# Rebuilding the opening of a fused attention and SwiGLU kernel: dummy products, a fixed order for four tiles, a shorter load front, and a merged unit for the cross blocks

## The chip, the cores and the metric

The kernel runs on one core of a Trainium2 chip. Times are device microseconds (us) of one execution. A quoted time is the median of several runs, and a ratio is the mean time of one kernel's fast runs over the mean time of the other kernel's fast runs in the same rounds on the same chip, so it isn't quite the ratio of the medians. "Span" is the length of the profiled execution as the trace has it; it is about 2 us shorter than the device time of the same run.

In the traces the clock granted to TensorE reads 1.00 or, in some stretches, 0.50. A product of 512 columns starts every 216 ns or every 415 ns; these are called full and half rate here. A group of four such products takes 0.86 or 1.66 us, and this is how the two states are told apart below.

## The reference

Attention over 8 batches of 576 positions, 8 heads of 64, each query looking back at most 127 positions with a linear bias, then a SwiGLU feed-forward network (FFN) over all 4608 rows.

```python
# q, k, v: (8, 8, 576, 64)
scores = (q @ k.T) / 8 + bias            # bias = -slope[h] * |i - j|
mask   = (i - j >= 0) & (i - j < 128)
x      = softmax(where(mask, scores, -1e9)) @ v     # -> (4608, 512)
# w_gate, w_val: (512, 1536), w_out: (1536, 512)
g   = x @ w_gate
out = (g * sigmoid(g) * (x @ w_val)) @ w_out        # fp32
```

## The kernel before

Two batches form a super-batch of nine units: four full tiles of 128 positions for each batch (576 = 4 x 128 + 64), and one corner tile that holds the last 64 rows of both. The FFN works in blocks of 512 rows: 12 gate groups and 12 value groups of four products each, then four output groups of 12 products. The output groups of one block run beside the gate and value groups of the next, and so do the attention tiles for later blocks. Four attention tiles must be done before the FFN can start, and these and the first FFN block are the opening that the change rebuilds.

All loads go through one queue that GpSimd feeds, and convert fp32 to fp16 on the way. The corner tile (rank 4) is loaded in two pieces of 64 rows, and it belongs to the first five tiles loaded:

```python
    def source(src, rank):
        s, c = divmod(rank, 9)
        if c == 4:                                # corner: two pieces of 64 rows
            return [((64 * n, 64 * n + 64),
                     src[2 * s + n, :, 512:576, :].rearrange("h p d -> p h d")) for n in range(2)]
    # ... cut
    load_qk(0, "kq")
    for r in range(4):
        load_qk(r + 1, "q")
        load_v(r)
        load_qk(r + 1, "k")
    load_w(0, 128)
    load_w(128, 512)          # gate and value weights by columns
    load(5)
    load_v(4)
    load_w(512, 1024)
    load(6)
    load_w(1024, 1536)
    load(7)
    load(8)
    # ... then wo_sb, the output weights, in two halves
```

Transposes, scores, weighted sums and the transposes of x all share one pool of four PSUM banks, `ps_a`. The FFN has its own four, which stand empty until it starts:

```python
    ps_f = ctx.enter_context(tc.tile_pool(name="ps_f", bufs=3, space=PSUM))   # gv x3, po x1
    ps_a = ctx.enter_context(tc.tile_pool(name="ps_a", bufs=4, space=PSUM))   # attention
    # ... cut
        pt = ps_a.tile([P, 4, P], FP16, name="pt", tag="a")
        for j in range(4):
            nc.tensor.transpose(pt[:, j, :], t_[:, 2 * j:2 * j + 2, :], idm)
        nc.vector.tensor_copy(dst[:, :, c * P:(c + 1) * P], pt)
```

The corner's queries need scores against tile 3 of the first batch, tile 3 of the second and the corner itself. Before, the first two of these ride along as the second 128 columns of units 3 and 7, with masks of their own (`lo`, `hi`), and unit 8 computes only the corner against itself.

The softmax here doesn't subtract the row's maximum and nothing guards it: scores larger than these inputs give would overflow.

Of the kernel before, what the change touches and what calls it, by code (L numbers as in the profile page):

```python
# [15 lines left out]
P = 128  # L16
WIN = 128
QK_DMA_FROM = 14
X_DMA_FROM = 99
FIRST = 4  # L20
# [21 lines left out]
def kernel(  # L42
# [24 lines left out]
    nc.sync.dma_start(idm, idm_d.ap())  # L67
    reg_d = nc.inline_tensor(make_mask(H), name="mask_reg")
    reg = consts.tile([P, H, 256], FP16, name="m_reg")
    nc.sync.dma_start(reg, reg_d.ap())  # L70
    lo = consts.tile([P, H, 256], FP16, name="m_lo")
    hi = consts.tile([P, H, 256], FP16, name="m_hi")
    com = consts.tile([P, H, 128], FP16, name="m_com")

    def make_lo():

        nc.vector.memset(lo[:, :, 192:256], 0.0)
        nc.vector.tensor_copy(lo[:, :, 0:192], reg[:, :, 0:192])

    def make_hi():  # L80

        nc.vector.memset(hi[:, :, 128:192], 0.0)
        nc.vector.tensor_copy(hi[:, :, 0:128], reg[:, :, 0:128])
        nc.vector.tensor_copy(hi[:, :, 192:256], reg[:, :, 128:192])

    def make_com():

        nc.vector.memset(com, 0.0)
        nc.vector.tensor_copy(com[0:64, :, 0:64], reg[0:64, :, 0:64])
        nc.vector.tensor_copy(com[64:128, :, 64:128], reg[64:128, :, 64:128])  # L90
# [18 lines left out]

    NV = 14  # L110
# [9 lines left out]

# [3 lines left out]

    def col_of(p):
        return p if p < 4 else (p + 1 if p < 8 else 4)
# [4 lines left out]
    def source(src, rank):  # L131

        s, c = divmod(rank, 9)
        if c == 4:
            return [((64 * n, 64 * n + 64),
                     src[2 * s + n, :, 512:576, :].rearrange("h p d -> p h d")) for n in range(2)]
        b, t = (2 * s, c) if c < 4 else (2 * s + 1, c - 5)
        return [((0, P), src[b, :, t * P:(t + 1) * P, :].rearrange("h p d -> p h d"))]
# [17 lines left out]
    def transposed(name, rank):  # L156

        s, c = divmod(rank, 9)
        t_, dst = (natk.pop(rank), kTs[s]) if name == "k" else (natq.pop(rank), qTs[s])
        pt = ps_a.tile([P, 4, P], FP16, name="pt", tag="a")  # L160
        for j in range(4):
            nc.tensor.transpose(pt[:, j, :], t_[:, 2 * j:2 * j + 2, :], idm)
        nc.vector.tensor_copy(dst[:, :, c * P:(c + 1) * P], pt)

    def transposes(rank):
# [4 lines left out]
        if rank >= QK_DMA_FROM:  # L170
            cols = slice(c * P, (c + 1) * P)
            for t_, dst in ((natk.pop(rank), kTs[s]), (natq.pop(rank), qTs[s])):
                nc.sync.dma_start_transpose(
                    dst[:, :, cols], t_.rearrange("p h d -> p (h d)"))
            return
        for name in ("kq" if c == 0 else "qk"):
            transposed(name, rank)
# [3 lines left out]
    def scores(i):  # L181

        s, p = units[i]
        c = col_of(p)
        kcols = slice(c * P, (c + 1) * P)
        kT, qT = kTs[s], qTs[s]
        if p == 8:
            banks = [ps_a.tile([P, 4, P], FP32, name="psc", tag="a") for _ in range(2)]
            for j in range(4):
                for par in range(2):  # L190
                    rows = slice(64 * par, 64 * par + 64)
                    nc.tensor.matmul(banks[par][:, j, :], kT[rows, j, kcols], qT[rows, j, kcols],
                                     start=(j == 0), stop=(j == 3))
            er = epool.tile([P, H, P], FP16, name="exrc", tag="exrc", bufs=1)
            e = epool.tile([P, H, P], FP16, name="exc", tag="exc", bufs=1)
            ex[(s, p)] = e

            er4 = er.rearrange("k (a par b) q -> k a par b q", a=2, par=2)

            def act(par):  # L200
                nc.scalar.activation(er4[:, :, par], banks[par].rearrange("k (a b) q -> k a b q", a=2),
                                     AF.Exp, scale=scale)

            return [[lambda: act(0)],
                    [lambda: act(1), lambda: nc.vector.tensor_mul(e, er, com)], [], []]

        banks = []
        for q4 in range(2):
            two = [ps_a.tile([P, 2, 256], FP32, name="ps", tag="a") for _ in range(2)]
            banks.append(two)  # L210
            for j in range(2):
                pair = 2 * q4 + j
                if p == 7:
                    parts = [(0, slice(8 * P, 9 * P)), (P, slice(4 * P, 5 * P))]
                else:
                    parts = [(0, slice(c * P, (c + 2) * P))]
                for n, (o, cols) in enumerate(parts):
                    w = cols.stop - cols.start
                    for par in range(2):
                        rows = slice(64 * par, 64 * par + 64)  # L220
                        nc.tensor.matmul(two[par][:, j, o:o + w], kT[rows, pair, kcols],  # L221
                                         qT[rows, pair, cols],
                                         start=(j == 0 and n == 0),
                                         stop=(j == 1 and n == len(parts) - 1))
        er = epool.tile([P, H, 256], FP16, name="exr", tag="exr", bufs=2)
        if p in (3, 7):
            e = epool.tile([P, H, 256], FP16, name="exl", tag="exl", bufs=2)
        else:
            e = epool.tile([P, H, 256], FP16, name="ex", tag="ex", bufs=3)
        ex[(s, p)] = e  # L230
        m = lo if p == 3 else hi if p == 7 else reg
# [5 lines left out]
        def mul(q4):  # L237
            o = slice(4 * q4, 4 * q4 + 4)
            nc.vector.tensor_mul(e[:, o, :], er[:, o, :], m[:, o, :])  # L239

        return [[lambda: act(0, 0)], [lambda: act(0, 1), lambda: mul(0)],
                [lambda: act(1, 0)], [lambda: act(1, 1), lambda: mul(1)]]

    xs = {}

    def weighted(i):
# [4 lines left out]
        for half in range(2):  # L251
            av = ps_a.tile([P, 4, D + 1], FP32, name="av", tag="a")
            todo = []
            for j in range(4):
                h = 4 * half + j
                if p == 8:
                    todo.append((j, ex[(s, 3)][:, slot(h), 128:256], va[9 * s + 3][:, h, :]))
                    todo.append((j, ex[(s, 7)][:, slot(h), 128:256], va[9 * s + 8][:, h, :]))
                    todo.append((j, ex[(s, 8)][:, slot(h), :], va[9 * s + 4][:, h, :]))
                else:  # L260
                    if p not in (0, 4):
                        todo.append((j, ex[(s, p - 1)][:, slot(h), 128:256],
                                     va[9 * s + col_of(p - 1)][:, h, :]))
                    todo.append((j, ex[(s, p)][:, slot(h), 0:128], va[9 * s + col_of(p)][:, h, :]))
# [14 lines left out]
    def x_transposed(i):  # L279
# [9 lines left out]
        pt = ps_a.tile([P, NKB, P], FP16, name="px", tag="a")  # L289
        for kb in range(NKB):  # L290
            nc.tensor.transpose(pt[:, kb, :], x[:, kb * P:(kb + 1) * P], idm)  # L291
# [54 lines left out]
    need_rank = [9 * s + r for s in range(NSUP) for r in (1, 2, 3, 4, 6, 7, 8, 8, 8)]  # L346
# [8 lines left out]
    def transposes_to(r):  # L355
        nonlocal done_t
        while done_t <= min(r, NR - 1):
            transposes(done_t)
            done_t += 1

    def ahead(i):

        r = min(need_rank[min(i + 4, last)], loaded - 1)
        if r >= QK_DMA_FROM:
            transposes_to(r)

    def attention():

        transposes_to(need_rank[0])
        for steps in scores(0):  # L370
            for f in steps:
                f()
        yield 0
        for i in range(last + 1):
            after = [[], [], [], []]
            if i < last and i != FIRST - 1:
                transposes_to(need_rank[i + 1])
                after = scores(i + 1)
            if i == 1:
                make_lo()  # L380
            if i == 5:
                make_hi()
                make_com()
            for fs in after:
                for f in fs:
                    f()
                yield i
            weighted(i)
            yield i
            if i >= FIRST:  # L390
                loads_to(i + 7)
                ahead(i)
# [4 lines left out]
            if i == FIRST - 1:  # L397

                transposes_to(need_rank[i + 1])
                for fs in scores(i + 1):  # L400
                    for f in fs:
                        f()
                    yield i + 1
# [7 lines left out]
    for r in range(4):  # L411
        load_qk(r + 1, "q")
        load_v(r)
        load_qk(r + 1, "k")
    load_w(0, 128)
    load_w(128, 512)
    load(5)
    load_v(4)
    load_w(512, 1024)
    load(6)  # L420
    load_w(1024, 1536)
# [8 lines left out]
    done = n_att = step = 0  # L430
# [10 lines left out]
    while done < ready[0]:  # L441
        att_step()
    base = n_att
    for _ in ffn():
        step += 1
        if step < 24:
            blk, target = 0, base + 2 * max(0, step - 8)
        else:
            blk = min(NBLK - 1, 1 + (step - 24) // 36)
            target = base + 32 + (step - 24) * RATE * 8 / 36  # L450
# [32 lines left out]
```

## Time and profile before

| | before |
|---|---|
| time, median (range) | 375.73 us (375.66 to 376.59, 3 runs) |
| span | 373.8 us |
| TensorE busy | 351.6 us, 94% of the span |
| share of the chain that ended last that is TensorE | 72% |
| FFN starts | 30.11 us |
| first output product (`po`) | 62.98 us |

TensorE is near its bound over the whole kernel; what can still be won is time near the start. The lines themselves are shown in the prediction. In a timeline line the columns are start, length, engine, line of the kernel, operation, output and inputs, shape, count, and in brackets the idle time before it and what released it.

### The profile page before, as it was taken

The numbers are of one execution on the slowest core, as the hardware profiler recorded it, in microseconds if no ns is written. First come the engines' busy times: TensorE is split into PE (matmuls) and PEld (weight loads), VectorE is DVE, ScalarE is ACT, GpSimd is POOL, SyncE is SP. The second block draws the span as 40 slices with busy tenths as digits, with TensorE's granted clock in tenths as the row PEclk, the third lists the DMA queues.
The fourth block names the chain that finished last, engine by engine and source line by source line (L and its number), as shares of the span: only waits on it lengthen the run. The fifth ranks groups of instructions, "written<-read, shape, count | busy, mean of one in ns | idle before, by whom it ended". The sixth has DMA issues, their size and how long they took to land.

```text
span 373.8 us, 6285 instructions
## 1 busy us (share of the span) xinstructions
PE 351.6 (94%) x2416; PEld 170.4 (46%) x2416; DVE 235.9 (63%) x471; ACT 173.4 (46%) x317; POOL 108.6 (29%) x134
## 2 busy tenths in 40 slices
PE   1789799999999999999999999999999999999995
PEld 1454345554445544444454444444454444444442
DVE  3765788765876488556865687568744833853540
ACT  1542475536655565456644575466433332332321
POOL 8966648755563654470000000000000000000000
PEclk9999999999999999999999999999999999999999
DMA  9999999999999999999001300010011002001013
GB/s 143 143 162 190 179 188 140 113 119 147 159 155 172 158 217 142 143 153 220 2 30 56 44 0 25 33 59 0 3 58 56 0 30 79 5 30 56 28 29 86
DMA packets 147806, 35.05 MB, mean 94 GB/s; under 512 B 138432, under 2 KB 143040, under 8 KB 147776
## 3 DMA queue, kind: packets, MB, share of 16 engines
q0 software_dynamic: 118304, 18.88, 77.2%
q1 hardware_dynamic: 29472, 15.77, 20.9%
q8 instruction: 19, 0.31, 0.4%
q14 instruction: 11, 0.09, 0.1%
HBM read 38.31 MB, written 9.44 MB: 128 GB/s over the span
## 4 chain that ended last, share of the span: by engine, by line
PE 72%; DVE 8%; DMA 7%; ACT 6%; POOL 4%; issue 2%; DVEq 0%; POOLq 0%
PE po L326 24%; PE pv L312 19%; PE pg L302 18%; ACT exr L235 5%; DMA qn<-in_q_dram 3%; PE ps L221 3%; PE av L266 3%; DMA wg_sb<-in_moe_w_gate_dram 3%; PE px L291 2%; DVE uu L307 2%; DVE hT L314 2%; DVE ex L239 2%; DMA kn<-in_k_dram 1%; POOL qn L149 1%; DVE x L269 1%
## 5 line engine op out<-in xcount | busy, mean ns | idle before, releaser
L307 DVE SCALAR_TENSOR_TENSOR uu<-tt,pg 128x512 f16<-128x512 f16 x108 | 74.0, 685 | 65.6 <-ACT tt L305 65.5
L312 PE MATMUL pv<-xT,wv_sb 128*128 128x512 f16 x432 | 113.5, 380 | 1.3 <-DVE uu L307 1.0
L302 PE MATMUL pg<-xT,wg_sb 128*128 128x512 f16 x432 | 112.4, 381 | 0.7 <-DMA va<-in_v_dram 0.7
L326 PE MATMUL po<-wo_sb,hT 128*128 128x512 f16 x432 | 103.5, 379 | 0.0
L305 ACT ACTIVATE tt<-pg 128x512 f16<-128x512 f32 x108 | 65.2, 603 | 80.3 <-PE pg L302 78.1
L314 DVE TENSOR_TENSOR hT<-uu,pv 128x512 f16<-128x512 f16 x108 | 74.1, 686 | 8.9 <-PE pv L312 1.1
L235 ACT ACTIVATE exr<-ps 128x512 f16<-128x512 f32 x128 | 67.0, 606 | 24.8 <-PE ps L221 24.8
L302 PEld LDWEIGHTS <-wg_sb 128*128 128x128 f16 x432 | 40.6, 98 | 45.7 <-issue 3.5
L312 PEld LDWEIGHTS <-wv_sb 128*128 128x128 f16 x432 | 40.5, 98 | 45.7 <-issue 4.6
L326 PEld LDWEIGHTS <-hT 128*128 128x128 f16 x432 | 40.1, 98 | 44.1 <-issue 1.9
L143 POOL DMA_DIRECT2D va<-in_v_dram x40 | 34.1, 865 | 48.2 <-PE av L266 41.9
L330 ACT ACTIVATE osb<-po 128x512 f32<-128x512 f32 x36 | 21.6, 600 | 56.1 <-PE po L326 56.0
L239 DVE TENSOR_TENSOR ex<-exr,m_reg 128x1024 f16<-128x1024 f16 x48 | 33.0, 689 | 19.0 <-ACT exr L235 18.9
L149 POOL DMA_DIRECT2D qn<-in_q_dram x40 | 34.0, 852 | 25.7 <-DMA qT<-qn 17.7
L149 POOL DMA_DIRECT2D kn<-in_k_dram x40 | 34.2, 857 | 24.8 <-DMA kT<-kn 17.3
L292 ACT COPY xT<-px 128x512 f16<-128x512 f16 x36 | 21.0, 585 | 33.9 <-PE px L291 33.6
L269 DVE TENSOR_TENSOR x<-av,rec 128x256 f16<-128x256 f32 x72 | 29.1, 420 | 0.8
L221 PE MATMUL ps<-qT,kT 64*128 64x256 f16 (+1 forms) x288 | 24.9, 274 | 0.3
L266 PEld LDWEIGHTS <-ex 128*128 128x128 f16 x384 | 19.1, 101 | 8.8 <-issue 2.4
L291 PE MATMUL px<-idm,x 128*128 128x128 f16 x144 | 19.3, 230 | 3.7 <-DVE x L269 3.0
L266 PE MATMUL av<-va,ex 128*128 128x65 f16 x384 | 20.9, 199 | 0.8 <-ACT exr L235 0.6
L291 PEld LDWEIGHTS <-x 128*128 128x128 f16 x144 | 10.1, 99 | 20.5 <-DVE x L269 17.0
(35 smaller groups left out, 115.0 us busy)
## 6 DMA issues: line engine op xcount, KB each, us to landing
out_dram<-osb SPq DMA_DIRECT2D x32, 256.0 KB, 2.1
kn<-in_k_dram POOLq DMA_DIRECT2D x32, 128.0 KB, 7.0
qn<-in_q_dram POOLq DMA_DIRECT2D x32, 128.0 KB, 7.1
va<-in_v_dram POOLq DMA_DIRECT2D x32, 128.0 KB, 7.3
wo_sb<-in_moe_w_out_dram POOLq DMA_DIRECT2D x2, 768.0 KB, 11.8
wg_sb<-in_moe_w_gate_dram POOLq DMA_DIRECT2D x2, 512.0 KB, 10.5
wv_sb<-in_moe_w_val_dram POOLq DMA_DIRECT2D x2, 512.0 KB, 11.6
out_dram<-osb SPq DMA_DIRECT2D x8, 128.0 KB, 2.4
```

Source lines behind the costliest of these rows:

```text
L149: nc.gpsimd.dma_start(t_[p0:p1], src)
L221: nc.tensor.matmul(two[par][:, j, o:o + w], kT[rows, pair, kcols], qT[rows, pair, cols], start=(j == 0 and n == 0), stop=(j == 1 and n == ...
L235: nc.scalar.activation(er[:, o:o + 2, :], banks[q4][par], AF.Exp, scale=scale)
L239: nc.vector.tensor_mul(e[:, o, :], er[:, o, :], m[:, o, :])
L266: nc.tensor.matmul(av[:, j, :], w, val, start=(n == 0), stop=(n == len(todo) - 1))
L291: nc.tensor.transpose(pt[:, kb, :], x[:, kb * P:(kb + 1) * P], idm)
L302: nc.tensor.matmul(pg, wg_sb[:, kb, ms], xT[n][:, kb, :], start=(kb == 0), stop=(kb == NKB - 1))
L305: nc.scalar.activation(tt, pg, AF.Tanh, scale=0.5)
L307: nc.vector.scalar_tensor_tensor(out=uu, in0=tt, scalar=1.0, in1=pg, op0=ALU.add, op1=ALU.mult)
L312: nc.tensor.matmul(pv, wv_sb[:, kb, ms], xT[n][:, kb, :], start=(kb == 0), stop=(kb == NKB - 1))
L314: nc.vector.tensor_mul(hT[(n, m)], uu, pv)
L326: nc.tensor.matmul(po, hT[(n, m)][:, j * P:(j + 1) * P], wo_sb[:, m, :], start=(m == 0), stop=(m == NMB - 1))
```

## The change

The intent is to start the FFN earlier, and to start it at full clock. It has five parts:

1. Twelve dummy products before the first data lands, and the transposes of the first four tiles done twice, to keep the clock up.
2. The first four tiles in a fixed order on TensorE, VectorE and ScalarE, in place of the scheduler's.
3. Banks of the FFN's pool for the transposes, weighted sums and x of these tiles.
4. The corner tile becomes rank 8 and leaves the front of the loads. v0 goes behind k1, and q5 before the second weight piece.
5. All three blocks of the corner's queries go into unit 8, each 128 wide; units 3 and 7 shrink to 128.

Beside these, the pacing of the attention changed: the score products of a unit became a step of their own, and in the first FFN block the attention sets in more slowly.

The diff, cut to its core:

```diff
+    def busy(n):
+        t_ = ps_f.tile([P, 512], FP32, name="nil", tag="po", bufs=1)
+        for _ in range(n):
+            nc.tensor.matmul(t_, idle[:, 0:P], idle, start=True, stop=True)
 ...
-        pt = ps_a.tile([P, 4, P], FP16, name="pt", tag="a")
-        for j in range(4):
-            nc.tensor.transpose(pt[:, j, :], t_[:, 2 * j:2 * j + 2, :], idm)
+        if rank < FIRST:
+            pt = ps_f.tile([P, 4, P], FP16, name="pt", tag="gv" if name == "k" else "po",
+                           bufs=3 if name == "k" else 1)
+        else:
+            pt = ps_a.tile([P, 4, P], FP16, name="pt", tag="a")
+        for _ in range(2 if rank < FIRST else 1):
+            for j in range(4):
+                nc.tensor.transpose(pt[:, j, :], t_[:, 2 * j:2 * j + 2, :],
+                                    idm if rank < FIRST else idm2)
 ...
+        if p == 8:
+            return sum([scores_128(s, kt, 8, (s, "c", n), msk[n]) for n, kt in enumerate((3, 7, 8))], [])
+        if p in (3, 7):
+            return scores_128(s, p, p, (s, p), reg[:, :, 0:P])
 ...
     load_qk(0, "kq")
-    for r in range(4):
-        load_qk(r + 1, "q")
-        load_v(r)
-        load_qk(r + 1, "k")
+    load_qk(1, "qk")
+    load_qk(2, "q")
+    load_v(0)
+    load_qk(2, "k")
+    load_qk(3, "q")
+    load_v(1)
+    load_qk(3, "k")
+    load_v(2)
+    load_v(3)
     load_w(0, 128)
     load_w(128, 512)
-    load(5)
-    load_v(4)
+    load(4)
+    load_qk(5, "q")
     load_w(512, 1024)
+    load_qk(5, "k")
+    load_v(5)
+    load_w(1024, 1536)
     load(6)
-    load_w(1024, 1536)
     load(7)
     load(8)
 ...
+        busy(WARM)                                      # WARM = 12
+        with tc.manual_schedule(engines=ENGINES[MANUAL]):   # PE, DVE, Activation
+            first_tiles()
+            done = FIRST
+            steps = enumerate(ffn(), 1)
+            while next(steps)[0] < ALONE:               # ALONE = 8: gates and values 0 to 3
+                pass
+            nc.scalar.copy(idm2, idm)
```

## The prediction

The forecast's sum: 5.25 less 0.7 gives 4.6, with 0.3 it is 4.9, and 375.7 - 4.9 = 370.8. The 372 of rival (b) is that sum with a cost at half rate added.

> **What bounds the kernel now.** I read the page first (busy tenths, chain), then the windows of the first 60 us, then the timelines of TensorE and GpSimd there, because the change touches only how the kernel opens.
>
> From the page, the busy tenths of TensorE and DMA, in 40 slices of 9.35 us, and the chain that ended last by engine:
>
> ```profile
> PE   1789799999999999999999999999999999999995
> ...
> DMA  9999999999999999999001300010011002001013
> ...
> PE 72%; DVE 8%; DMA 7%; ACT 6%; POOL 4%; issue 2%; DVEq 0%; POOLq 0%
> ```
>
> TensorE is full from the fourth slice to the end, except in the fifth. The chain is TensorE for 72%; what isn't TensorE lies in the opening. DMA is full for the first 19 slices. So every us by which TensorE's dense part starts earlier is a us off the end, but only if the data is there: two limits meet in the opening.
>
> TensorE's timeline there (start, length, engine, line, operation, count, idle before and its releaser):
>
> ```profile
> 19.24 1.06 PE L266 MATMUL av<-va,ex 128*128 128x65 f16 x16
> ...
> 30.11 1.86 PE L302 MATMUL pg<-xT,wg_sb 128*128 128x512 f16 x4 [0.67 <-DMA va<-in_v_dram]
> 31.77 1.32 PE L312 MATMUL pv<-xT,wv_sb 128*128 128x512 f16 x4
> 32.93 1.03 PE L302 MATMUL pg<-xT,wg_sb 128*128 128x512 f16 x4
> 33.79 1.03 PE L312 MATMUL pv<-xT,wv_sb 128*128 128x512 f16 x4
> ...
> 44.37 0.40 PE L162 MATMUL pt<-idm,qn 128*128 128x128 f16 x4 [1.93 <-DMA qn<-in_q_dram]
> ```
>
> Three things are to be seen. The FFN starts at 30.11, after four attention tiles that take about 5 us each. The first four gate products take 31.77 - 30.11 = 1.66 us, 415 ns each; later four take 33.79 - 32.93 = 0.86 us, 216 ns each: TensorE ran at half rate until about 32.5, though the granted clock reads 1.00. The two first groups lost 2.82 - 1.73 = 1.1 us to it. And at 42.4 TensorE stood for 1.93 us for a q tile. The chain in order of time says why, and the windows give the rates (the last two numbers are the mean share of the DMA engines, summed over queues, and GB/s as written):
>
> ```profile
> 21.55 10.71 DMA wg_sb<-in_moe_w_gate_dram
> 32.26 0.28 issue
> 32.54 11.78 DMA qn<-in_q_dram
> ```
>
> ```profile
> 8.00:10.00 2.00, 0.71 (x6) 0.45 (x7) 1.53 (x5) 0.00 (x0) 2.00 (x3) 1.00 2.42 154
> ...
> 36.00:38.00 2.00, 2.00 (x11) 0.93 (x10) 1.48 (x3) 0.87 (x2) 2.00 (x3) 1.00 1.32 203
> ```
>
> The queue serves transfers roughly in order: q, k and v tiles (128 KB as written) at 154 GB/s, 0.86 us each, equal to the 0.87 us that GpSimd takes to issue one; weight pieces of 512 KB at 203 GB/s, 2.6 us each. That q tile took 11.78 us because 1 MB of weights stood ahead of it.
>
> [...] A q, k or v row of one head is 64 fp32, 256 bytes, and moves at 154 against 203 GB/s. [...] The kernel uses 4 + 3 + 1, so four attention buffers were all that the opening had, while the FFN's four stood empty.
>
> **The change part by part.**
> *Dummies.* 12 products of 512 columns at half rate are 12 x 0.42 = 5 us, from about 1.2 to 6.2 or less: done when the first k tile lands (6.29). Cost nothing.
> *Loads.* The corner tile (k, q and v of the last 64 rows of two batches) leaves the front; v0 goes behind k1. The front is now 12 tiles, the first at 6.29, then each 0.87 later: k1 8.9, q3 12.4, k3 14.1, v3 15.9.
> *Fixed order and own banks.* I walked the instructions in their new order with the durations of before (copy 0.34 apart on VectorE, mask product 0.61, reciprocal and x 0.5 a half, exp 0.5 apart, transposes at full rate 57 ns, so eight cost what four did). Scores of tiles 0 to 3 start at 9.2 (q1 copied), 11.5, 13.9 and 16.9; the last mask product ends at 19.4, the last av near 20.8, x at 21.5, its transpose and copy at 22.8. VectorE, with 2.9 us a tile in order, sets this pace. So the FFN can start near **22.8**, 7.3 us earlier, and without the 1.1 us at half rate. If the clock does not hold, TensorE's doubled transposes make about 4.3 us a tile and the FFN starts near 26 to 26.5, then still with the 1.1 us.
> *Cross blocks.* Columns are the same: 8x256 + 16x128 + 8x128 before, 40x128 after; exps and mask products have the same total. At 69 and 41 ns a product, 0.1 us more in each of four rounds: nothing.
> *Doubled transposes, a second identity, masks.* 32 more transposes in the opening, beside waits. The second identity only keeps later transposes from being moved into the fixed part.
>
> **Where the gain ends.** In the new order the transposes for the sixth tile need the q tile number 6 (counted from 0), and it stands behind all of the gate and value weights. Before, the wait at 42.4 was for the eighth q tile in the queue; up to it went 23 tiles and 3 MB of weights. After, the eighth q tile (number 7) again has 23 tiles and the same 3 MB up to it, so it should land at 44.3 again. Number 6 has three transfers fewer in front (itself is followed by a v, a k and that q): 44.3 - 3 x 0.87 = **41.7**. TensorE, from 22.8: four gate/value pairs 6.9 us (29.7); gate 4, which needs a piece landing near 30.4 (back from 41.7 by 2 tiles, 1 MB, 2 tiles and 512 KB), so 31.3; 12 transposes 0.7; value 4 waits for 33.0, ends 33.9; gate 5, a score group 0.55, value 5, gate 6, value 6: 37.9; k transposes 0.2. Then it waits from 38.1 to 41.7, **3.6 us**. Had the FFN started at 26, the wait would be about 1 us and the resumption the same 41.7: the opening's gain is cut off by the DMA stream.
>
> The sum: before resumes at 44.37 with 11 groups of four done (to gate 5), after at 41.7 with 14 (to value 6). That is 2.7 + 3 x 0.86 = 5.25 us; less 12 transposes not yet done (corner k and q, and k6: 0.7) gives **4.6**. Behind 41.7 the next transfers (q at 44.3, output weights near 50 and 55.6) are due at 47, 54 and 56 by the same walk: no further wait over a few tenths. Before loses some 2.4 us of its 21.6 us between 44.4 and 66 to waits for banks and exps; I give the new order 0.3 us of that. Gain 4.9: 375.7 - 4.9 = **370.8**.
>
> **Rivals.**
> *(a) The opening's gain comes through whole:* 7.3 + 1.1 + 1.9 (the wait of before gone) = 10.3, a time near 365.5. For it: TensorE is 72% of the chain. Against: the weights alone need 15.7 us of queue (3.1 MB at 200 GB/s, an estimate from the windows) and the tiles 20 us, so little can be earlier than before. Some of it if transfers land earlier than in my count.
> *(b) The long wait throttles the clock,* [...]: 372. In before 1.93 us of idling did not do it (products of 0.86 a group right after 44.8).
> *(c) The clock falls in the opening* [...]: the FFN starts after 26, cold, but mostly inside the wait for q6: 371 to 372.
> *(d) The new unit spoils the steady part:* six cross banks in a pool of four, and attention spread thinner (ten steps a tile against eight, same rate). Before loses only about 3.4 us of TensorE in 50 to 350, so there is little to win and perhaps 1 to 3 to lose: up to 373.5.
>
> **Range and chances.** The queue fixes the centre within about 1 us; (b), (c) and (d) lie above, (a) below. 80%: 367.5 to 373.5. Faster by 2% means below 368.2, which needs most of (a): 0.15. Slower by 2% (over 383) needs something not seen: 0.02.
>
> **What would show it.** Right: FFN start at 22 to 24 and its first products at 216 ns; DMA still full for some 60 us; a TensorE wait of 3 to 4 us near 38 to 42, released by a q transfer; the first output product near 54 against 62.98; afterwards the same spacing as before, end near 369. Wrong: no such wait (then (a)), products of 415 ns after it (b) or at the FFN start (c), TensorE idle over 5 us in 60 to 350 (d).

## The result, and the profile after

The changed kernel takes 370.75 us (median of 4 runs, 369.96 to 371.68) against 375.7 us (4 runs, 374.91 to 376.59) for the kernel before in the same rounds. The ratio is 0.9869 with a 95% interval of 0.9832 to 0.9905: 1.3% faster, within 2%. The profiled span went from 373.8 to 369.7 us.

From the page of the changed kernel: the busy tenths in 40 slices of 9.24 us, and the chain by engine.

```profile
PE   7789699999999999999999999999999999999995
...
PEclk9989999999999999999999999999999999999999
DMA  9999999959999999999991003100000011001014
...
PE 83%; DMA 6%; POOL 4%; ACT 3%; DVE 2%; issue 2%; POOLq 0%
```

TensorE is busy from the first slice on, since the dummies count as busy time. The fifth slice (37 to 46 us) is still the one with a hole in it. The granted clock, 9 everywhere before, has an 8 in the third slice.

TensorE's timeline of the changed kernel:

```profile
1.19 4.57 PE L115 MATMUL nil<-idle 128*128 128x512 f16 x12 [1.19 <-DVE idle L79]
...
8.94 0.61 PE L220 MATMUL ps<-qT,kT 64*128 64x256 f16 x8 [0.52 <-DVE qT L173]
...
22.17 1.86 PE L320 MATMUL pg<-xT,wg_sb 128*128 128x512 f16 x4 [0.67 <-ACT xT L310]
23.83 1.79 PE L330 MATMUL pv<-xT,wv_sb 128*128 128x512 f16 x4
25.45 1.03 PE L320 MATMUL pg<-xT,wg_sb 128*128 128x512 f16 x4
...
37.52 0.39 PE L171 MATMUL pt<-idm,kn 128*128 128x128 f16 x4
40.65 0.40 PE L171 MATMUL pt<-idm,qn 128*128 128x128 f16 x4 [2.74 <-DMA qn<-in_q_dram]
40.88 1.03 PE L320 MATMUL pg<-xT,wg_sb 128*128 128x512 f16 x4
...
53.63 0.81 PE L344 MATMUL po<-wo_sb,hT 128*128 128x512 f16 x3
```

Five things are to be seen. The dummies end at 5.76. The first score group takes 0.61 us, where that of the kernel before (at 10.44) takes 1.25: the clock is up. The FFN starts at 22.17, 7.9 us earlier than before. But its first two groups take 25.45 - 22.17 = 3.28 us and not 1.73: **the clock fell just as the FFN began.** And at 37.9 TensorE stands for 2.74 us for q tile 6, before gate 7 can start at 40.88 (in TensorE's program order its transposes stand ahead of that gate).

The clock in windows of the changed kernel (busy time of TensorE, its weight loads, VectorE, ScalarE and GpSimd with counts; then the mean granted clock, the share of the DMA engines and GB/s):

```profile
18.30:21.70 3.40, 2.03 (x28) 1.26 (x27) 2.72 (x10) 1.34 (x3) 2.44 (x4) 1.00 1.69 174
21.70:25.10 3.40, 2.93 (x7) 0.99 (x7) 0.40 (x1) 1.02 (x2) 2.40 (x4) 0.54 1.98 176
```

The first of these stretches ends half a us before the FFN starts. TensorE was busy in it for 2.03 us, in short pieces with no gap over 0.7 us. In the next 3.4 us the clock was granted at 0.54; the trace's clock events put the half rate from 21.95 to 25.36. The busy share alone does not explain the fall. Around the wait for q6, from 39.01 to 42.43, TensorE was busy for only 1.78 us, and around its wait in the kernel before, from 42.60 to 46.01, for only 1.64 us, and the clock stayed up both times. In time busy, those stretches hold mostly products of 512 columns (from 40.88 and from 44.83 on); the one before the FFN holds only transposes of x and weighted sums of 65 columns. Which property decides is not isolated by any run.

The chain of waits, in order of time, again runs through one long transfer into the wait:

```profile
26.48 14.12 DMA qn<-in_q_dram
```

**Where the time came from.** The first FFN block ends, and the second starts, at 63.91 us after and 65.97 before, 2.06 us earlier. By then 24 output products of the first block are done after, and 7 before: 17 x 0.216 = 3.67 us more. The attention work done by then is the same (scores of nine units, eight weighted tiles). So the lead is 2.06 + 3.67 = 5.7 us at that point, while the spans differ by 4.1 us. **The rest of the kernel gives back some 1.6 us.** It does not idle more: between 80 and 330 us TensorE is busy 248.2 of 250 us after and 247.2 before. Its score products take longer, which the windows of those tiles from 70 to 340 us show (`psc` blocks of 128 columns first, then `ps`, mostly 256; the first column after the comma is TensorE's busy time, the second ScalarE's). Before:

```profile
70.00:340.00 270.00, 1.19 (x24) 3.25 (x6) 1.00 0.83 82
...
70.00:340.00 270.00, 15.77 (x212) 50.07 (x96) 1.00 0.83 82
```

After:

```profile
70.00:340.00 270.00, 5.96 (x120) 16.25 (x30) 1.00 0.82 81
...
70.00:340.00 270.00, 12.38 (x136) 37.31 (x72) 1.00 0.82 81
```

That is 16.96 us before and 18.34 us after, 1.4 us more. The ends of pipelined products are modelled, so this is a pointer rather than a proof. The starts show it better. Before, then after:

```profile
45.69 1.03 PE L302 MATMUL pg<-xT,wg_sb 128*128 128x512 f16 x4
46.65 0.61 PE L221 MATMUL ps<-qT,kT 64*128 64x256 f16 x8
47.20 0.39 PE L312 MATMUL pv<-xT,wv_sb 128*128 128x512 f16 x1
```

```profile
53.63 0.81 PE L344 MATMUL po<-wo_sb,hT 128*128 128x512 f16 x3
54.37 0.40 PE L251 MATMUL psc<-qT,kT 64*128 64x128 f16 x8
54.70 0.66 PE L283 MATMUL av<-va,ex 128*128 128x65 f16 x16
```

A group of eight score products starts about 0.1 us late: four FFN products at 216 ns end at 46.55, and the group starts at 46.65. (Over the traces its first product starts 312 ns after the FFN product ahead of it, where a further FFN product starts after 216 ns.) It then holds TensorE for 0.55 us with 256 columns, but for 0.33 us with 128. Half the columns cost 0.42 us in place of 0.65, and not half. Behind the start of the second block the traces have 30 unbroken groups of score products before and 40 after, for the same columns. Counted from start to start up to the last product, scores take 18.1 us before and 20.2 after, 2.1 us more. Weighted sums, x and transposes give 1.2 us back, and the FFN products are spaced 0.7 us wider in sum; together this is the 1.6 us. The ninth experiment (g1) tries the unit alone.

### The profile page after: what moved, and what is told of

Its sections match the earlier page's. It is cut to its first block, busy times and chain, and to the rows that moved or that the text cites. A ratio compares the mean times of both kernels' runs of the same rounds, so it can differ in the third digit from the quotient of the medians.

```text
span 369.7 us, 6440 instructions
## 1 busy us (share of the span) xinstructions
PE 353.0 (95%) x2492; PEld 169.4 (46%) x2492; DVE 236.5 (64%) x471; ACT 175.2 (47%) x318; POOL 108.5 (29%) x134
## 4 chain that ended last, share of the span: by engine, by line
PE 83%; DMA 6%; POOL 4%; ACT 3%; DVE 2%; issue 2%; POOLq 0%
PE po L344 25%; PE pv L330 23%; PE pg L320 23%; PE av L283 4%; DMA qn<-in_q_dram 4%; PE ps L220 3%; PE px L309 3%; DMA wv_sb<-in_moe_w_val_dram 2%; PE psc L251 2%; ACT exr L225 2%; POOL kn L152 1%; POOL va L146 1%; PE pt L171 1%; POOL qn L152 1%; DVE uu L325 1%
## 5 line engine op out<-in xcount | busy, mean ns | idle before, releaser
L344 PE MATMUL po<-wo_sb,hT 128*128 128x512 f16 x432 | 106.0, 379 | 0.1
L225 ACT ACTIVATE exr<-ps 128x512 f16<-128x512 f32 x96 | 50.4, 606 | 21.0 <-PE ps L220 20.9
L286 DVE TENSOR_TENSOR x<-av,rec 128x256 f16<-128x256 f32 x72 | 29.9, 421 | 1.0
L255 ACT ACTIVATE exrc<-psc 128x512 f16<-128x512 f32 x40 | 21.5, 601 | 3.9 <-PE psc L251 3.8
L283 PEld LDWEIGHTS <-ex 128*128 128x128 f16 x384 | 17.8, 97 | 8.1 <-DVE x L286 2.1
L309 PE MATMUL px<-idm,x 128*128 128x128 f16 x144 | 18.4, 221 | 1.5 <-ACT xT L310 0.7
```

The lines of the kernel that those rows point to most:

```text
L225: nc.scalar.activation(er[:, o:o + 2, :], banks[q4][par], AF.Exp, scale=scale)
L283: nc.tensor.matmul(av[:, j, :], w, val, start=(n == 0), stop=(n == len(todo) - 1))
L309: nc.tensor.transpose(pt[:, kb, :], x[:, kb * P:(kb + 1) * P], idm if i < FIRST else idm2)
L344: nc.tensor.matmul(po, hT[(n, m)][:, j * P:(j + 1) * P], wo_sb[:, m, :], start=(m == 0), stop=(m == NMB - 1))
```

## The experiments

Twelve kernels ran, on three chips, each beside runs of the kernel before (375.72, 375.87 and 375.34 us); all gave correct results. "Gate 7" is the first FFN group behind the wait for q tile 6.

| kernel | median us | ratio (95%) | FFN start | wait for q6 | gate 7 | first `po` | span |
|---|---|---|---|---|---|---|---|
| changed kernel | 370.75 | 0.9869 (0.9832 to 0.9905) | 22.17 | 2.74 | 40.88 | 53.63 | 369.7 |
| e1_delay | 372.96 | 0.9925 (0.9898 to 0.9953) | 25.79 | none | 41.71 | 54.45 | 370.5 |
| e2_q6_early | 369.80 | 0.9835 (0.9808 to 0.9861) | 22.35 | none | 38.27 | 51.00 | 367.0 |
| e3_no_dummies | 370.24 | 0.9852 (0.9824 to 0.9880) | 22.82 | 0.48 | 39.02 | 51.75 | 367.8 |
| e4_corner_first | 376.54 | 1.0011 (0.9985 to 1.0037) | 22.59 | 3.24 | 43.19 | 57.56 | 373.6 |
| f0_after_again | 370.66 | 0.9868 (0.9840 to 0.9896) | 23.06 | 0.77 | 40.69 | 53.43 | 369.5 |
| f1_full_front | 373.26 | 0.9933 (0.9901 to 0.9965) | 22.86 | 1.37 | 41.17 | 53.91 | 369.9 |
| f2_q6_plain | 370.67 | 0.9855 (0.9831 to 0.9879) | 23.65 | none | 40.58 | 53.32 | 369.4 |
| f3_q6_warm | 370.34 | 0.9855 (0.9826 to 0.9884) | 22.39 | none | 37.02 | 50.05 | 367.9 |
| g1_cross_alone | 376.68 | 1.0041 (1.0019 to 1.0063) | 29.19 | other order | – | 61.93 | 373.9 |
| g2_free_order | 373.37 | 0.9938 (0.9915 to 0.9961) | 28.03 | none | 43.69 | 56.39 | 372.3 |
| g3_shared_banks | 369.94 | 0.9882 (0.9844 to 0.9920) | 23.37 | 1.41 | 39.19 | 51.93 | 368.0 |
| g4_wo_early | 367.19 | 0.9783 (0.9765 to 0.9801) | 22.07 | none | 36.31 | 49.05 | 365.1 |

One execution of each kernel has its trace kept, and FFN start to span come from it. It isn't always a middle one: the changed kernel's span of 369.7 us is the longest of its four (368.0 to 369.7), those of e2, e3 and f1 are the shortest of theirs, and f2's is the longest. So two traces can differ by more or less than the medians.

One regularity carries the reading of the table. From gate 7 to the first output product it is 12.70 to 12.75 us in every variant of the changed kernel except f3 (13.03) and e4 (14.37); from there to the end of the span it is 315.9 to 316.1 us in every one except f3 (317.85). Both exceptions are explained below. **So in these traces, whatever the opening does, the end follows the start of gate 7 one for one.** The start of the FFN, which the change aims at, is not in that sum.

The theory under test was that the load queue, through q tile 6, decides how much of the opening's gain arrives. The rivals were that the clock decides it, that the start of the FFN decides it, and that the new unit costs the difference.

### e1_delay: start the FFN later

```diff
-WARM = 12
+WARM = 30
```

> The changed kernel with 30 dummy products in place of 12, nothing else: TensorE's order is the same behind them. 18 x 0.216 us = 3.9 us more in front, of which about 2.6 us reach the first scores (they waited for the third tile's copy until 8.94 anyway), so the FFN should start near 24.8 in place of 22.2. Theory 1 (the load queue decides: the q tile that the sixth attention tile needs lands near 40.6 whatever TensorE did before): the 2.74 us wait shrinks to about 0.2 us, TensorE goes on at 40.6 to 41 as before, the time changes by less than 0.6 us. Rival 1 (the start of the FFN decides): 2.6 us longer, about 373.4.

The 18 further dummies moved the FFN's start more than I had reckoned, by 3.62 us:

```profile
25.79 1.29 PE L320 MATMUL pg<-xT,wg_sb 128*128 128x512 f16 x4 [0.67 <-ACT xT L310]
...
41.71 1.03 PE L320 MATMUL pg<-xT,wg_sb 128*128 128x512 f16 x4
```

Gate 7 came only 0.83 us later, and the span grew by 0.8 us: 2.8 us of the delay were swallowed by the wait. The median rose by 2.2 us, more than I had expected (under 0.6), partly because the delay was longer than the wait could hide. The profiled run also had the shortest time of its six, whose spans reach 371.7, and the changed kernel's was its longest. The direction fits the theory; the number was a miss.

### e2_q6_early: the q tile ahead of the last weights

```diff
+    load_qk(6, "q")
     load_w(1024, 1536)
-    load(6)
+    load_qk(6, "k")
+    load_v(6)
```

> The changed kernel with one load moved: the q tile number 6 goes ahead of the last third of the gate and value weights. TensorE's order is the same. Theory 1: it lands near 35, the wait of 2.74 us at 37.9 goes; the weight pieces land 0.87 later, which should just be in time (gate 8 is needed near 40, value 8 near 42), so 2 to 2.7 us shorter than the changed kernel, near 368.3. If the weights are late by some tenths, the gain is less by that. Rival 1 (FFN start): no change, 370.7. If a wait for weights of 2 us or more takes its place, the queue's total and not its order is the limit.

The wait is gone, although the FFN starts no earlier (22.35) and its first groups are as slow as before:

```profile
38.04 0.39 PE L171 MATMUL pt<-idm,qn 128*128 128x128 f16 x4
38.27 1.03 PE L320 MATMUL pg<-xT,wg_sb 128*128 128x512 f16 x4
```

Gate 7 starts 2.6 us earlier and the span is 2.7 us shorter. Moving one load of 128 KB is worth this much between these two traces, and about 1 us in the medians. By time alone that is not clear of the noise, since the intervals of the two ratios overlap; the vanished wait is what carries it. The trace is also the best of e2's five runs: its mean granted clock is 0.995, where the other four have 0.988 to 0.991 and spans of 367.8 to 368.1.

### e3_no_dummies: no dummies, transposes once

```diff
-WARM = 12
+WARM = 0
 ...
-        for _ in range(2 if rank < FIRST else 1):
+        for _ in range(1):
```

> The changed kernel without the dummy products and with each transpose of the first four tiles done once, as in the kernel before: the part of the change that is to hold the clock is taken out. TensorE's order is otherwise the same. The opening should run at half rate (score groups of 8 in 1.1 us against 0.55), the FFN start near 23.5 to 24.5. Theory 1: hidden in the wait for the q tile, the time changes by less than 0.5 us. Rival 1, or rival 2 (the clock is what the change gained): 1.5 to 2.5 us longer.

Now the opening runs cold at first:

```profile
9.10 1.04 PE L220 MATMUL ps<-qT,kT 64*128 64x256 f16 x8 [0.70 <-DVE qT L173]
```

A score group takes 1.04 us in place of 0.61. Yet the FFN starts at 22.82, 0.65 us later, and the time is no worse: 370.24 against 370.75 us. At about 15 us TensorE came to full rate without them (four k transposes take 0.61 us at 12.59, 0.45 at 15.11, and the score group of 128 columns at 17.02 takes 0.40 as in the changed kernel), and at the FFN's start the clock fell as there (granted at 0.52 from 22 to 24 us). **The dummies and the doubled transposes, the part that gives the change its name, buy nothing that can be measured behind this wait.**

### e4_corner_first: the corner's q and k back in the front

```diff
+    load_qk(8, "qk")
     load_v(3)
 ...
-    load(8)
+    load_v(8)
```

> The changed kernel with the corner tile's k and q loaded ahead of the last v and the weights again, as in the kernel before; TensorE's order is the same. Two tiles of 0.87 us more stand in front of all weights and of the q tile. Theory 1: the q tile lands 1.7 us later, the wait grows from 2.7 to 4.4 us and the time by 1.7 us, near 372.4. Rival 1: the FFN start moves little (its weights were there with time to spare), no change.

The delay came, and more than twice as large as expected: 3.9 us in the span and 5.8 us in the medians (376.54 us), which is all of the change's gain.

```profile
42.96 0.40 PE L171 MATMUL pt<-idm,qn 128*128 128x128 f16 x4 [3.24 <-DMA qn<-in_q_dram]
43.19 1.40 PE L320 MATMUL pg<-xT,wg_sb 128*128 128x512 f16 x4
44.38 1.91 PE L330 MATMUL pv<-xT,wv_sb 128*128 128x512 f16 x4
```

Two effects add up. The q tile landed 2.3 us later than in the changed kernel. And after this wait of 3.24 us the clock fell: the granted clock from 43 to 47 us was 0.59, and the way from gate 7 to the first output product took 14.37 in place of 12.74, 1.6 us more. So the prediction's rival (b), a clock that falls after the long wait, was seen, but in this kernel and not in the changed one, where it read 1.00 after the 2.74 us. The length of the wait may not be the only difference. In the traces of both kernels the clock events lie whole multiples of 3.41 us apart (at 4.88, 21.95 and 25.36 us in the changed kernel), and the windows of e4 fit this spacing (granted at 0.71 from 43.5 to 44, 0.50 to 47 and 0.88 to 47.5, so half rate from about 43.7 to 47.1). On that grid the wait of 2.74 us is cut in two (TensorE busy for 2.08 us from 35.60 to 39.01 and for 1.78 us from 39.01 to 42.43), while most of e4's lies in one piece (busy for 0.75 us from 40.30 to 43.71). So that the changed kernel escaped may be luck in part; no run moves the wait along the grid.

### f0_after_again: the changed kernel once more

No edit; it ran to see how far two runs of the same code differ.

> The changed kernel once more, unaltered, to stand beside the next runs on the same chip, since its first four executions fell into two groups (spans of 369.4 to 369.7 and 368.0). Ratio to before 0.985 to 0.990, and a q tile that lands between 38.8 and 40.7, where the earlier runs had it. FFN start at 22.2, a clock of one half from 22 to 25.3.

The time is the same (370.66 us), and so is gate 7's start (40.69 against 40.88), but the FFN started 0.9 us later, and the wait was 0.77 and not 2.74 us: the start slid into the wait, as in e1. The spans of its six runs reach from 368.1 to 370.9 us. This spread is why I lean on the medians only for differences over 1 us.

### f1_full_front: the same bytes as e4, in full tiles

```diff
+    load_qk(7, "qk")
     load_v(3)
 ...
-    load(7)
+    load_v(7)
```

> The changed kernel with the k and q of tile 7 (two full tiles of 128 rows) in front of the last v and of the weights, in the places that the corner's k and q (four pieces of 64 rows, the same bytes) had in the run with the corner first. TensorE's order is the same. If only the bytes in front count: the q tile lands 1.7 us later than in the changed kernel, end 1.7 us later, and nothing less than in the run with the corner first. If the pieces of 64 rows slow the queue beyond their bytes (the windows of 15 to 20 us read 128 and 140 GB/s in the two kernels that have them in front, 177 to 193 in those that do not): about 1.7 us here against 2.3 to 4 there, and 170 to 190 GB/s from 15 to 20 us.

The q and k of tile 7 are as many bytes as those of the corner, but in pieces of 128 rows. The q tile 6 landed by 40.94, not at 42.96, and the ratio is 0.9933, not 1.0011. The rates of the queue from 10 to 22 us, in 40 slices of 0.3 us, first e4, then f1:

```profile
GB/s 152 156 153 154 156 152 155 154 149 154 147 148 150 149 143 183 123 106 96 99 128 151 124 172 148 170 172 129 79 102 113 128 143 143 177 131 113 125 156 154
```

```profile
GB/s 142 156 152 155 156 152 155 156 154 155 156 154 152 155 155 205 142 140 138 147 165 169 172 167 159 153 170 156 163 181 177 198 195 195 197 200 202 202 197 182
```

They are close up to 14.8 us; then e4 falls to between 79 and 130 for stretches, where f1 never goes below 138. From 15 to 20 us e4 moved 128 GB/s, f1 166 and the changed kernel 177; the kernel before and g1, with their corner in front, moved 140 and 136. The two ran on different chips, and part of e4's loss is the clock, so the ratio alone isn't the price of the pieces. Nor is f1 cheap by time: its median is 2.6 us above that of f0 on the same chip, more than the 1.7 us expected for its bytes, and its trace is the shortest of its six. The rates support that **the corner's 64-row pieces cost the queue more than their bytes**.

### f2_q6_plain: e2 and e3 together

```diff
-WARM = 12
+WARM = 0
 ...
-        for _ in range(2 if rank < FIRST else 1):
+        for _ in range(1):
 ...
+    load_qk(6, "q")
     load_w(1024, 1536)
-    load(6)
+    load_qk(6, "k")
+    load_v(6)
```

> Both edits that cost nothing together: q tile 6 ahead of the last third of the weights, no dummy products and single transposes. Without the wait the opening is no longer hidden, so the half-rate part should show now: FFN start near 22.8 against 22.4 of the kernel with q tile 6 early, end 0.2 to 0.5 us later than there, ratio near 0.984. If it is equal or faster, the dummies and doubled transposes do nothing for this kernel in any order of loads.

The ratio, 0.9855, is a little above e2's 0.9835, and the intervals overlap. In the profiled run gate 7 came 2.3 us later than in e2: the FFN started 1.3 us later, its first four groups lost 1.0 us more at half rate, and no wait was left to hide it. The profiled run was the slowest of its six in span (367.9 to 369.4). So with the load out of the way the dummies may be worth some tenths of a us; this pair does not settle it.

### f3_q6_warm: e2 with a clock that holds

Eight dummies between the last transposes of x keep TensorE busy up to the FFN's start.

```diff
+    def keep(n):
+        t_ = ps_f.tile([P, 512], FP32, name="nil", tag="gv")
+        for _ in range(n):
+            nc.tensor.matmul(t_, idle[:, 0:P], idle, start=True, stop=True)
 ...          # keep(2), keep(3), keep(3) after the transposes of x 1, 2 and 3
+    load_qk(6, "q")
     load_w(1024, 1536)
-    load(6)
+    load_qk(6, "k")
+    load_v(6)
```

> The kernel with q tile 6 early, and eight more dummy products of 512 columns in the places between the last tiles and the FFN where TensorE waited (after the transposes of x of tiles 1, 2 and 3), so that the clock does not fall at 22. They fit into the waits of 0.67 us. The two first FFN groups should then take 0.86 us each in place of 1.6: FFN start near 22.4 to 22.6, everything behind it 1.2 to 1.5 us earlier than with q tile 6 early alone, near 368.3 and a ratio of 0.980, unless the weight piece for value 4 (it landed near 31.0) takes 0.2 to 0.5 us back. If the clock falls all the same, no change.

In the trace the clock held. The window before the FFN and two lines of the timeline:

```profile
18.30:21.70 3.40, 3.26 (x41) 1.85 (x38) 2.94 (x10) 1.17 (x2) 2.62 (x4) 1.00 1.75 180
```

```profile
22.39 1.02 PE L326 MATMUL pg<-xT,wg_sb 128*128 128x512 f16 x4
...
54.10 0.38 PE L350 MATMUL po<-wo_sb,hT 128*128 128x512 f16 x1 [1.67 <-DMA wo_sb<-in_moe_w_out_dram]
```

TensorE was busy for 3.26 of the 3.4 us, where it had been for 2.03. Gate 7 started at 37.02, 1.25 us before e2's. But the time did not fall: 370.34 us where I had expected 368.3. At 52.4 TensorE now waited 1.67 us for the second half of the output weights, which lie last in the queue (it also waited 0.23 us for q7). The gain had run into the next load. Nor did the clock hold in every run: the mean granted clock of three of the six is 0.990 to 0.993, against 0.998 in the trace. Where it fell in those, no trace shows.

### g1_cross_alone: only part 5 of the change, on the kernel before

```diff
         if p == 8:
-            banks = [ps_a.tile([P, 4, P], FP32, name="psc", tag="a") for _ in range(2)]
-            ...                                         # the corner against itself
+            return sum([scores_128(s, kt, 4, (s, "c", n), msk[n]) for n, kt in enumerate((3, 8, 4))], [])
+        if p in (3, 7):
+            return scores_128(s, c, c, (s, p), reg[:, :, 0:P])
```

> The kernel before with only the combined cross unit of the change (tiles 3 and 7 with 128 columns, three cross blocks in the ninth unit); loads, scheduled opening, banks and clock as before. The corner is no longer needed for tile 3, but its loads stay in front. If the unit does nothing for the steady part: the FFN starts within 1 us of 30.1, the TensorE wait for the eighth q tile stays near 44.4, the time within 0.7 us of before. If it spoils the steady part (rival d): 1 to 3 us longer. If it is where the gain comes from: near 371.

The ratio is 1.0041 with an interval wholly above 1: the unit alone **costs** 0.4%, 1.5 us. Part of that is the clock: three of its six runs, at a mean granted clock of 1.00, have spans of 373.9 to 374.2, the other three, at 0.995 to 0.997, of 375.4 to 376.3 (the kernel before: 372.3 to 374.7 at 0.998 to 1.00). The trace, at 1.00, separates this. Its opening was no worse (it resumed behind the wait for its q tile at 43.51 us, where the kernel before does at 44.37). From the start of the second block to the last product it takes 302.8 us, as the kernel before does, but with 12 output products already done and not 7: **the unit costs 5 x 0.216, about 1.0 us, behind the opening.** Its score products took 5.96 + 12.86 = 18.82 us from 70 to 340 us against 16.96 before, 1.9 us more; from start to start behind the opening it is 19.8 us against 18.1, in 35 groups against 30.

### g2_free_order: the scheduler orders the first tiles again

```diff
-        with tc.manual_schedule(engines=ENGINES[MANUAL]):
+        with nullcontext():
```

> The changed kernel with the order of the first four tiles left to the scheduler, as in the kernel before; its loads, banks, dummies and cross unit stay. If the queue decides (theory 1), the opening may cost up to 1 to 2 us more and end after 24 without much change, since TensorE waits 0.8 to 2.7 us for the q tile anyway: the time within 1 us of the changed kernel. If the fixed order is what gained: near 374.

I had expected this to stay within 1 us, because the wait would hide it. It cost 2.6 us. The FFN starts at 28.03, which is later than the wait can make up for: no wait for q6 is left, and gate 7 starts at 43.69.

```profile
23.04 0.61 PE L171 MATMUL pt<-idm,kn 128*128 128x128 f16 x4 [2.55 <-DMA kn<-in_k_dram]
```

At least 2.55 of the 5.9 us are a wait for a load again: the scheduler put the transposes of the fifth tile, whose k was issued behind the first weights, ahead of the last weighted sums. The clock then stood at half rate from 22.35 to 32.59. The fixed order earns its place, here also by keeping a tile that hasn't landed out of the opening.

### g3_shared_banks: the first tiles' banks back in the common pool

```diff
-        if rank < FIRST:
+        if False:
...
-            pool, tag = (ps_f, "gv") if i < FIRST else (ps_a, "a")
+            pool, tag = (ps_a, "a")
...
-        pool, tag, n = (ps_f, "po", 1) if i < FIRST else (ps_a, "a", 4)
+        pool, tag, n = (ps_a, "a", 4)
```

> The changed kernel with the first four tiles' transposes, av products and x transposes back in the four attention banks of PSUM; TensorE's order and the loads are the same. The opening should slow down: each score group waits for banks again, the FFN start moves to 25 to 28. Up to about 1 to 2.7 us of that is hidden in the wait for the q tile; what is beyond it shows in the end one for one. So with an FFN start at 26, about 1.5 to 3 us longer than the changed kernel; with one at 24, no change.

```profile
23.37 1.02 PE L320 MATMUL pg<-xT,wg_sb 128*128 128x512 f16 x4 [0.67 <-ACT xT L310]
```

The FFN starts 1.2 us later, but the clock held in this run (granted at 1.00 from 20 to 30 us), and there was still a wait of 1.41 us for q6. The time is 369.94 us (one of the six runs took 374.76) and the ratio 0.9882, whose interval takes in the changed kernel's: the separate banks buy nothing that can be measured behind this wait.

### g4_wo_early: f3, and the output weights moved forward

```diff
     load_qk(6, "k")
     load_v(6)
-    load(7)
-    load(8)
-    ...                       # output weights here
+    load_qk(7)
+    ...                       # output weights here, both halves
+    load_qk(8)
+    load_v(7)
+    load_v(8)
```

> The kernel with q tile 6 early and the clock held at the FFN start, plus both halves of the output weights ahead of the v of tiles 7 and 8 and the corner: they stood 3.5 us later in the queue, and TensorE waited 1.67 us for the second half there. Theory 1: that wait goes, no other of over 0.5 us comes, end 1.2 to 1.7 us earlier than there: a profiled span near 366.3, about 368.9 as a median, ratio 0.981. If the total of the queue and not its order were the limit, the corner or v7 would be waited for instead and nothing gained.

```profile
36.31 1.03 PE L326 MATMUL pg<-xT,wg_sb 128*128 128x512 f16 x4
...
49.05 0.81 PE L350 MATMUL po<-wo_sb,hT 128*128 128x512 f16 x3
```

The median is 367.19 us and the ratio 0.9783 (0.9765 to 0.9801), with spans of 365.1 to 365.4 in its four runs. This beats both kernels: 2.2% under the kernel before, though whether it is over 2% is just open by the interval. Gate 7 starts 4.6 us before the changed kernel's and the span is 4.6 us shorter. From 20 to 60 us the trace shows TensorE waiting for no load any more, and the first output product comes at 49.05.

## Why the prediction was right or wrong

The total was right: 370.8 predicted, 370.75 measured, and inside the range. Of its steps some held and some failed, and the failures cancelled: the range was earned by the bound, the hit to 0.05 us is luck.

**The bound: held, with one correction.** The prediction said that the opening's gain is cut off by the DMA stream, at q tile 6. The wait was there, released by a q transfer, and e1 (FFN 3.6 us later, gate 7 0.8 later), e2 (load alone, 2.6 us between the traces) and e3 (cold opening, no loss) show that it decided. g2 shows the limit of this: once the opening is late by more than the wait, it counts again, so both bounds lie close together.

**The FFN's start: held in time, failed in state.** 22.8 was predicted, 22.17 and 23.06 seen in two profiles. But the prediction had it "without the 1.1 us at half rate", and the first two groups lost 3.28 - 1.73 = 1.55 us. It was rival (c) in another form: the clock stayed up through the opening and fell at its end, where TensorE has only transposes and narrow products, busy for 60% of the time (2.03 of 3.4 us), while VectorE finishes the last tile. In the traces of f3 and g4, where dummies fill those gaps, it stayed up (1.00 from 20 to 25 us), but it did so in g3's without them (TensorE busy for 1.97 of 3.4 us before the FFN, from 19.4 to 22.8). What decides is open, since stretches with less busy time kept the clock (1.78 and 1.64 of 3.4 us, above).

**The walk from 22.8 to 37.9: right sum of two wrong terms.** The prediction had full clock and waits of 0.7 and 1.0 us for weights at gate 4 and value 4. These waits did not occur, since the weights came sooner than by its count; the half rate took their place (1.7 against 1.55 us). Value 6 ended, and the k transposes stood, at 37.5 to 37.75 where 37.9 was predicted.

**The landing of q tile 6: mechanism right, size off by 1 us.** 41.7 was predicted and 40.65 seen. In the trace kept, the step that failed is "44.3 - 3 x 0.87". The q tile 7 did land almost where the count of bytes had it, at 44.06 (issued at 32.56, 11.5 us to landing), but number 6 landed 3.46 us ahead of it and not 2.6, since the three transfers that follow it took longer than 0.87 us each. With the landing 1 us early, the lead behind the wait was 44.37 - 40.65 + 3 x 0.86 - 0.7 = 5.6 us and not 4.6, and the wait 2.7 and not 3.6.

The count of bytes ("again has 23 tiles and the same 3 MB up to it, so it should land at 44.3 again") is not safe either. In the six traces with this order of loads (the changed kernel, e1, e3, f0, g2, g3) q7 landed between 41.6 and 44.1, and q6 between 38.7 and 40.6. That it can be so early fits that the corner's pieces of 64 rows cost more than bytes, for which the rates of f1 against e4 speak (stretches of 79 to 130 GB/s with the pieces in the queue, 138 to 202 without in the same stretch). Why they cost more is shown by no run. What causes the spread among equal load orders stays open.

**The steady part: failed.** The prediction called the merged unit "nothing", at 0.1 us in each of four rounds, and gave the new order 0.3 us of gain. In place of both, the lead shrank from 5.7 us at the second block to 4.1 at the end. That is rival (d), within its 1 to 3 us, and g1 shows the unit alone to cost 1.0 us in its trace (1.5 us, 0.4%, in the means). The step that failed is the price of the cross blocks, 69 and 41 ns a product: it leaves out what each group costs whatever its width, about 0.1 us before its first product and a last product that holds TensorE for 148 ns (128 columns) or 202 ns (256). With these, the corner's blocks cost some 0.3 us more a round, about 1.1 us in four, near the 1.0 of g1. (This is an estimate from the starts in the traces: five groups of 0.42 us after, against one of 0.68 with 256 columns, one of sixteen products of 0.74 and one of 0.42 before.) The other 0.6 us of the 1.6 belong to the new order or the pacing (nine steps a full tile in the code, not the ten of the prediction); no run separates these. The sign that the prediction named for (d), TensorE idle over 5 us from 60 to 350, would have missed it: TensorE was not idle but slower.

So the sum reads 5.6 or 5.7 us of lead less 1.6 us, 4.1 in the span, against 4.6 + 0.3 = 4.9 predicted; the medians give 375.7 - 370.75 = 4.95 us. The span is that of the longest of the four runs; two others, at 368.0, would give 5.8.

**Rivals.** (a), the whole gain, fell with the wait, but not because it is impossible: g4 got 8.7 us of span (373.8 - 365.1) out of the same opening, once the queue's order followed the order in which TensorE needs the tiles. (b) did not happen at 2.74 us and did in e4 at 3.24 us, where the wait also lay otherwise on the 3.41 us grid of the clock events.

## What to carry to other kernels

When an opening is rebuilt, look for the first wait behind it, and ask what would still wait if the opening took no time: here a single tile of 128 KB behind 1 MB of weights decided what arrived, and neither dummy products nor separate banks showed a gain behind it. (With the load moved, the dummies are not settled by f2, and the banks were not tried.) Sort a shared load queue by the time at which the busiest engine needs each piece, and move the next piece too, since a gain runs on into the next load (f3 against g4). Measure each part of a combined change alone: one of these five parts cost about 0.3 to 0.4%, two showed no gain behind the wait, and what remained came from the order of the tiles and of the loads.

## What the traces show of the clock, score groups and the queue

- In the changed kernel the clock fell behind a window of 3.4 us with TensorE busy for 2.03 us and no gap over 0.7 us; it held behind windows with 3.26 us (f3) and 1.97 us (g3). It also held behind windows with 1.78 and 1.64 us, spent mostly on products of 512 columns. How busy a window must be, or with what, is not isolated by any run.
- A group of four 128 x 128 transposes delays the next product by 0.23 us at full rate (40.65 to 40.88 in the changed kernel), 57 ns each, and by 0.43 us at half (16.28 to 16.71 in the kernel before): they slow down with the clock. Whether they keep it up was not isolated by any run.
- Clock events are missing at the start of both kernels' traces: that of the changed kernel has none until 4.88 us, that of the kernel before none until 32.36 us. Views of the latter read 1.00 up to there, though the first four FFN products took 415 ns each. There the duration of products is the better witness.
- For groups of score products (64 rows) between products of 128 rows, the first starts 312 ns after the product ahead of it, in place of 216, and the last of a group holds TensorE for 148 ns with 128 columns and 202 ns with 256.
- With 64-row pieces among full tiles in front of one queue, it moved 128 to 140 GB/s from 15 to 20 us (e4, g1, the kernel before); without them, 166 to 193 (f1, e1 and the other variants).
